# Normalised rows of seven groups turned by VectorE in 32x32 tiles, from pieces laid in place, where TensorE transposed them

## The chip, the core and the metric

The kernel runs on one core of a Trainium2 chip. The metric is the device time of one execution in microseconds (us). Engines are named as the profile names them: PE is TensorE (its weight loads are PEld), DVE is VectorE, ACT is ScalarE, POOL is GpSimd, SP is SyncE, which issues most of the transfers. A quadrant is 32 of the 128 partitions.

## What is computed

Linear attention, a Fourier mix over both axes, a layer norm without weights, and a two-layer network, all in float32; batch 8, 8 heads, 576 tokens, 64 features a head, so 512 features.

```python
k_s = softmax(k, axis=2)                     # over the tokens
kv = einsum('bhsd,bhse->bhde', k_s, v)
x = einsum('bhsd,bhde->bhse', softmax(q, axis=-1), kv)   # then (B, S, 512)
u = x + real(fft(fft(x, axis=1), axis=2))
un = (u - mean(u)) / sqrt(var(u) + 1e-06)    # over the 512 features
out = u + maximum(un @ w_ch1, 0) @ w_ch2     # 512 -> 2048 -> 512
```

## The kernel before

The 4608 rows are taken in nine groups of 512: group g (0 to 7) has 512 of the 576 rows of batch element g, and a last group, number 8, has the 64 left over of each. The order is 0 to 6, 8, 7. A position in this order is called an order below. For each group the network is done by Strassen products: a first layer (`up`, L1322; its products are L1334), one level deep, and a second (`down`, `deep_down`, L1383; products L1431 and L1461, and for order 1 L1550), two levels deep from order 2 on. While PE does the network of one group, the other engines and gaps in PE's row prepare the next group: keys, queries, values, the Fourier mix, and the norm. So there are hand-overs, at which PE goes from the last L1461 of one group to the first L1334 of the next.

The order of the work is written out by hand. Every step is put into one list with a time in units, the list is sorted (L1719), and each engine executes its own steps in that order; only data and buffers make it wait. One unit is a pair of products, and a group after the second one takes 56 units of `up` and 50 of `down`. `timed` (L1628) puts the parts of the preparation at their places, counted from the start of a group's `up` or `down`.

The norm (`norm`, L1156) works on four tiles of 128 rows by 512 features, u by another name x, in the order 0, 2, 1, 3:

- DVE takes statistics (L1165, L1166). ACT loads its table and takes the root of all four variances (L1169). DVE makes the scales and biases (L1172, L1173).
- ACT normalises a tile in one instruction, 128x512, with scale and bias read per row from memory (L1189).
- PE transposes it in four parts of 128x128 into PSUM (L1195), and ACT copies them from there into `unT` (L1204), which has the features on the partitions. A tile with number i = c + 2u fills half the columns of two of the blocks of `unT`.
- DVE and POOL make the differences that the Strassen products need (`combine`, L1210; `combine_last`, L1215). The second product of the next `up` reads block 5, the second of DVE's two differences. Then ACT loads the table of the exponential again (`back`, L1180).

`unT` has one buffer, `eo`, which holds the normalised tiles, has six.

Inside the second layer, products add up in PSUM banks ba, bb and bc, one buffer each. ACT copies the first product out of ba (s1, L1475) and later the sum in it (L1482); DVE reads bb for the sums u2, u3 and the result (L1468) and bc after them. A product that adds to bb, or starts a bank anew, waits for these reads. DVE also makes the sums of weights' counterparts for the next unit (L1407), POOL some of them, and adds results into x (L1411).

The keys of the next group but one (`keys`, L686) begin 7 units before a hand-over: key maxima on DVE (L695), exchanges between partitions on ACT and minima on DVE (L675, L678, L682), exponentials on ACT (L699), turns in 32x32 tiles on DVE (L708), products with the values on PE (L715), which `scale` (L721 to L725) divides. The queries go a like way: DVE turns them (L764), and ACT takes exponentials in 16 pieces of 32 partitions by 128 elements, each written to the quadrant where its features belong (L774). The new values of the other half are loaded by `values_to` (L648), the keys by `keys_to` (L638).

Of the kernel before, what the change touches and what calls it, by code (L numbers as in the profile page):

```python
# [40 lines left out]
F32 = mybir.dt.float32  # L41
I32, U32 = mybir.dt.int32, mybir.dt.uint32
ACT = mybir.ActivationFunctionType
ALU = mybir.AluOpType
AX = mybir.AxisListType

P = 128
B, H, S, DH = 8, 8, 576, 64
D = H * DH
# [3 lines left out]
HD = D // 2  # L53
# [5 lines left out]
Q = 32  # L59
W = 2 * Q  # L60
NT = Q // 2 + 1
KT = D // P
VD = 4 * NC - S // Q
NF = FF // P
GT = 4 * P
# [53 lines left out]
def at(t, script):  # L119
    return [(t + dt, step) for dt, step in script]  # L120
# [17 lines left out]
class _Block:  # L138
    def __init__(self, ctx, tc, q, kT, v, w1, w2, ft, cd, out):
# [24 lines left out]

        self.ZT = c.tile([P, KT, P], F32, name="ZT")

# [57 lines left out]
    def turned(self):  # L224
        t = self.ps.tile([P, 4, P], F32, tag="tr", name="tr", bufs=2)
        return t
# [102 lines left out]
    def weights(self):  # L329
# [6 lines left out]
        def fetch(i):  # L336
# [10 lines left out]
            if i < NF:  # L347
                nc.sync.dma_start(raw.rearrange("p (k n) -> p k n", k=KT), w1[:, :, f * 2 * P:(f + 1) * 2 * P])
            else:
# [129 lines left out]
    def attention_timed(self, b, start, end):  # L479

        tail = [("t", b)] if b % 2 == 0 else []
        own = [("q", b, c, u) for c, u in ((0, 0), (0, 1), (1, 1), (1, 0))]
        places, shared = [6, 13.5, 21.5, 27.2], start + 12
        if tail:
            places = [8.5, 14, 21.5, 27.2]
        if start == 0:
            places, shared = [13.5, 20.5, 24, 27.2], 7
        steps = at(start, self.keys(b))
        for it in tail:
            steps += at(shared, self.q_exp(it)) + at(shared + 8, self.t_turn(it))  # L490
            steps += at(22.4 if start < 0 else 35, self.t_fold(it))
        for t, it in zip(places, own):
            steps += at(t, self.own_exp(it)) + at(t + 15, self.own_times_kv(it))
        loads = [(t - 7, t + 7.6, self.own_load(it)) for t, it in zip(places, own)]
        loads += [(shared - 13, shared + 8.4, self.t_load(it)) for it in tail]
        loads.sort(key=lambda s: s[0])
        free = [-99] * 3
        for i, (t, end, load) in enumerate(loads):
            if i > 1:
                steps += at(max(t, free[-3]), load)  # L500
            free.append(end)
        return steps + at((33 if start < 0 else 39) if tail else max(22, start + 26), self.t_times_kv(b))

    def ahead(self, b):


        steps = at(24 if b > 2 else 20, self.keys_to(b))
        steps += at(35 if b > 2 else 22.5, self.values_to(b, 0))
        q = [self.own_load(("q", b, 0, u)) for u in range(2)]
        if b % 2 == 0:  # L510
            q = [self.t_load(("t", b)), q[0]]
        return steps + at(46.5, q[0]) + at(50, q[1])
# [170 lines left out]

        return [(0, copies), (0.3 + 0.15 * (4 // by), least)]

    def keys(self, b):  # L686


        nc, V, kb = self.nc, self.nc.vector, self.kb
        box = {}  # L690

        def top(r):
            if r == 0:
                box["m"] = self.small.tile([P, 4 * NR], F32, tag="km16", name="km16", bufs=2)
            V.reduce_max(box["m"][:, 4 * r:4 * r + 4], kb[:, r], axis=AX.X, negate=True)  # L695

        def exp(g):
            k = kb[:, g // 4, g % 4]
            nc.scalar.activation(k, k, ACT.Exp, bias=box["m"][:, g:g + 1])  # L699

        def turn(r):
            if r == 0:
                t = self.work.tile([P, KT, HD], F32, tag="Z", name="Z", bufs=1)
                t = t[:].rearrange("p k n -> p (k n)")[:, 0:NC * P]
            else:
                t = kb[:, r - 1].rearrange("p g s -> p (g s)")
            to = box["k", r] = t.rearrange("p (c n) -> p c n", n=P)
            V.transpose(to.rearrange("p c (g s) -> p c g s", s=Q), kb[:, r].rearrange("p g (c s) -> p c g s", s=Q))  # L708

        def times(r):  # L710
            pk, k = self.acc((P, P + 1)), box.pop(("k", r))
            box[r] = pk
            a = (P + 1) * (r % 2)
            for c in range(NC):
                nc.tensor.matmul(pk, lhsT=k[:, c, :], rhs=self.vt[:, c, a:a + P + 1], start=c == 0, stop=c == NC - 1)  # L715

        def scale(r):
            pk = box.pop(r)
            rec = self.small.tile([P, 1], F32, tag="krec", name="krec", bufs=4)
            at = P * (r % 2)  # L720
            V.tensor_scalar(out=rec[:], in0=pk[:, at:at + 1], scalar1=ATT_EPS, scalar2=None, op0=ALU.add)  # L721
            V.reciprocal(rec[:], rec[:])
            for h in range(2):
                s, cols = slice(64 * h, 64 * h + 64), slice(64 * h + 1 - r % 2, 64 * h + 65 - r % 2)
                V.tensor_scalar(out=self.kvr[b % 2][s, r, s], in0=pk[s, cols], scalar1=rec[s, 0:1], scalar2=None, op0=ALU.mult)  # L725

        steps = [(0.9 * r, lambda r=r: top(r)) for r in range(NR)]
        steps += at(3.6, self.across(lambda: box["m"], 2, 4 * NR)) + at(4.5, self.across(lambda: box["m"], 1, 4 * NR))
        steps += [(6 + g / 2, lambda g=g: exp(g)) for g in range(4 * NR)]
        for r in range(NR):  # L730
            for dt, f in ((8.3, turn), (10.8, times), (12.5, scale)):
                steps.append((dt + 2 * r + 6 * (r > 1 and f != turn), lambda f=f, r=r: f(r)))
        steps += at(13.5, self.values_to(b, 1))
        return steps

    def own_load(self, it):
# [419 lines left out]
    def norm(self, g):  # L1156

        nc, V = self.nc, self.nc.vector
        mv = self.small.tile([P, 4, 2], F32, tag="mv", name="mv", bufs=2)
        std = self.small.tile([P, 4], F32, tag="std", name="std", bufs=2)  # L1160
        uns, box = {}, {}
# [36 lines left out]
        def laid(i):  # L1198
# [4 lines left out]
            copy = V.tensor_copy if g == 0 and c == u else nc.scalar.copy  # L1203
            copy(self.unT[g][:, u:u + 3:2, :, cols], box.pop(i)[:].rearrange("p (a k) t -> p a k t", a=2))  # L1204

        def combine():
            if g > 0:
                some = lambda i: self.unT[g][:, i]
                for e, to, x, y in ((V, 4, 1, 0), (nc.gpsimd, 1, 3, 1), (V, 5, 3, 4)):
                    e.tensor_tensor(out=some(to), in0=some(x), in1=some(y), op=ALU.subtract)  # L1210
# [3 lines left out]
                some = lambda i: self.unT[g][:, i]  # L1214
                V.tensor_tensor(out=some(6), in0=some(2), in1=some(5), op=ALU.subtract)  # L1215

        steps = []
        put = lambda t, f, *a: steps.append((t, lambda: f(*a)))
        if g == 0:
            for some in ((0, 2), (1, 3)):  # L1220
                s = slice(some[0], 4, 2)
                for i in some:
                    put(0, stats, i)
                for f in (root, scales):
                    put(0, f, s)
        else:
            for n, i in enumerate((0, 2, 1, 3)):
                put((0.7, 2.7, 4.7, 6)[n], stats, i)
            s = slice(0, 4)
            put(7.2, root, s)  # L1230
            put(9, scales, s)
            put(13.6, back)
        for n, i in enumerate((0, 2, 1, 3)):
            put(9.3 + 1.3 * n, normal, i)
            put(11.8 + 1.3 * n, turn, i)
            put(12.6 + 1.3 * n, laid, i)
        put(17.5, combine)
        put(27.5, combine_last)
        return steps

    def plain(self, g, unT):
# [382 lines left out]
def kernel(ctx: ExitStack, tc: tile.TileContext, q, kT, v, w1, w2, ft,  # L1624
                                                           cd, out):
    blk = _Block(ctx, tc, q, kT, v, w1, w2, ft, cd, out)

    def timed(t, order, g):  # L1628
        b = order + 1
        steps = at(t, blk.up(order, g)) + at(t + UP, blk.down(g, order))  # L1630
        if order == B:
            return steps + [(t + 6 + 1.2 * i, lambda i=i: blk.later and blk.later.pop(0)()) for i in range(36)]
        if b == B:
            return steps + at(t + UP + 14, blk.norm(groups[b]))
        start, end = -7 if order > 2 else 0, 45
        if b + 1 < B:
            steps += at(t, blk.ahead(b + 1))
        steps += at(t, blk.attention_timed(b, start, end)) + at(t + end, blk.folded(b))
        t += UP
        for i, k in enumerate((2, 3, 0, 1, 4)):  # L1640
            steps += at(t + 2 + 2 * i, blk.block(b, k))
        mixes = [blk.mix_own(b, c) for c in range(2)]
        if b % 2:
            mixes.insert(0 if b == B - 1 else 2, blk.mix_shared(b // 2))
        for i, some in enumerate(mixes):
            steps += at(t + 12.5 + 3.2 * i, some)
        return steps + at(t + 29, blk.norm(groups[b]))

    fetch, convert = blk.weights()

# [26 lines left out]
    groups = [*range(B - 1), B, B - 1]  # L1677
    first, second, both = 46.9, 56, 77
    steps = blk.opening(fetch, converted)
# [3 lines left out]
    t = first + second  # L1683
# [26 lines left out]
    scale, before = 0.87, t + both  # L1710
    later = []
    t = 0
# [62 lines left out]
```

## Time and profile before

| what | value |
|---|---|
| median of three runs | 1055.6 us (1055.06 to 1058.19) |
| profiled execution | 1057.53 us, its span 1055.8 us |
| granted clock of PE over the span | 0.998 |
| busy: DVE, ACT, POOL | 722.6, 456.1, 406.0 us |
| PE transposes of the norms (L1195) | 144 of 128x128, 21.4 us of busy time, pipelined |
| normalising on ACT (L1189) | 34 tiles of 128x512, about 0.81 us each |
| copies to `unT` on ACT (L1204) | 34 tiles, 0.58 us each |
| hand-overs (first L1334 after L1461 or L1550) | 300.90, 414.82, 526.72, 638.79, 750.50, 863.01, 957.66 us |
| end of the scales before them (L1173) | 283.75, 403.16, 514.65, 627.13, 738.43, 851.24, 932.35 us |

The row of a group gives the line of the kernel, the engine, the operation, what is written and read, its shape and count; then its busy time and the mean ns of one, and the idle time of its engine just before with what ended it. A row of a timeline gives start and length in us, and in brackets the idle time before it.

### The profile page before, as it was taken

To read this page: it belongs to the slowest core of one execution; us is meant where nothing else is said; L and a number is where in the kernel's file an instruction comes from. 1 tells how busy PE (TensorE), PEld (TensorE's weight loads), DVE (VectorE), ACT (ScalarE), POOL (GpSimd) and SP (SyncE) were. 2 spreads that over 40 slices of the span, in tenths; PEclk is the share of its full clock that TensorE was granted. 3 is DMA by queue.
4 is the path that set the end of the run, shared out by engine and by line. 5 is a ranking of instruction groups with operands and counts; after the bars stand their busy time and mean duration, and the time that the engine had idled before them with its cause. 6 is when DMAs were issued, how large, how long until landed. Compare 5 with 4: busy or idle time off the path is not lost.

```text
span 1055.8 us, 16768 instructions
## 1 busy us (share of the span) xinstructions
PE 1037.7 (98%) x6178; PEld 899.8 (85%) x6178; DVE 722.6 (68%) x1410; ACT 456.1 (43%) x1141; POOL 406.0 (38%) x350
## 2 busy tenths in 40 slices
PE   8999999899999999999999999999999999999998
PEld 7844555788888899889998999989998998999898
DVE  6898888665566876767765777688657644674563
ACT  5674433672248316751476236821682132131210
POOL 3164320257415645465545643474446450000000
PEclk9999999999999999999999999999999999999999
DMA  9787598586998666855677467757644664576464
GB/s 269 240 281 258 164 257 273 167 251 197 300 308 242 206 217 243 230 190 210 251 236 220 179 239 238 206 201 260 212 170 162 229 243 165 206 259 221 173 222 147
DMA packets 114313, 236.01 MB, mean 224 GB/s; under 512 B 23272, under 2 KB 78696, under 8 KB 103608
## 3 DMA queue, kind: packets, MB, share of 16 engines
q1 hardware_dynamic: 113864, 234.42, 67.7%
q8 instruction: 49, 0.80, 0.3%
q14 instruction: 32, 0.26, 0.1%
q10 hardware_dynamic: 288, 0.26, 0.1%
q0 software_dynamic: 80, 0.26, 0.1%
HBM read 199.79 MB, written 39.06 MB: 226 GB/s over the span
## 4 chain that ended last, share of the span: by engine, by line
PE 78%; DVE 5%; ACT 4%; DMA 3%; issue 1%; SPq 0%; POOL 0%; DVEq 0%; ACTq 0%
PE bb L1334 14%; PE bb L1461 10%; PE ba L1334 10%; PE bc L1334 9%; PE bc L1461 7%; PE ba L1461 7%; PE bb L1431 5%; PE acc L715 3%; ACT qT L774 2%; PE bb L1550 2%; PE acc L790 2%; PE acc L1087 1%; PE acc L1090 1%; DMA vt<-in_v_dram 1%; PE bc L1550 1%; PE ba L1550 1%
## 5 line engine op out<-in xcount | busy, mean ns | idle before, releaser
L1334 PE MATMUL bb<-unT,big 128*128 128x256 f32 x768 | 183.1, 381 | 0.1
L1334 PEld LDWEIGHTS bb<-unT,big 128*128 128x128 f32 x768 | 144.7, 191 | 19.9 <-DVE u L1304 1.0
L1346 ACT ACTIVATE big<-big 128x512 f32<-128x512 f32 x96 | 60.3, 629 | 170.8 <-DVE big L1345 169.9
L1334 PE MATMUL ba<-unT,big 128*128 128x256 f32 x512 | 124.0, 379 | 0.2 <-ACT big L1341 0.2
L774 ACT ACTIVATE qT<-q 32x128 f32<-32x128 f32 x384 | 117.9, 307 | 12.1 <-DVE q L764 7.1
L1334 PE MATMUL bc<-unT,big 128*128 128x256 f32 x512 | 121.8, 380 | 0.5 <-DVE big L1345 0.5
L1304 DVE TENSOR_TENSOR u<-bb,s 128x512 f32<-128x512 f32 x66 | 45.4, 687 | 94.5 <-PE bb L1334 79.5
L1334 PEld LDWEIGHTS bc<-unT,big 128*128 128x128 f32 x512 | 96.1, 190 | 14.2 <-DVE big L1345 1.8
L1334 PEld LDWEIGHTS ba<-unT,big 128*128 128x128 f32 x512 | 94.8, 190 | 12.6 <-ACT big L1341 0.6
L1461 PE MATMUL bb<-big 128*128 128x128 f32 x848 | 105.1, 275 | 0.3 <-DVE u L1468 0.3
L1461 PEld LDWEIGHTS bb<-big 128*128 128x128 f32 x848 | 99.6, 192 | 0.5 <-DVE u L1468 0.4
L1411 POOL TENSOR_TENSOR x<-x,big 128x512 f32<-128x512 f32 x45 | 57.7, 1296 | 63.5 <-DVE big L1468 31.2
L1461 PE MATMUL ba<-big 128*128 128x128 f32 x640 | 79.6, 275 | 0.0
L1461 PEld LDWEIGHTS ba<-big 128*128 128x128 f32 x640 | 76.3, 192 | 1.2
L1407 DVE TENSOR_TENSOR big<-big 128x512 f32<-128x512 f32 x98 | 75.3, 806 | 0.0
L761 POOL TENSOR_TENSOR q<-q,qm 128x512 f32<-128x512 f32 x24 | 25.8, 1073 | 116.1 <-DVE qm L756 73.0
L1210 POOL TENSOR_TENSOR unT<-unT 128x512 f32<-128x512 f32 x8 | 14.1, 1769 | 124.6 <-DVE unT L1210 124.6
L1468 DVE TENSOR_TENSOR u<-bb,s 128x256 f32<-128x256 f32 x40 | 16.8, 420 | 64.8 <-PE bb L1461 61.5
L1431 PE MATMUL bb<-big 128*128 128x256 f32 x256 | 58.7, 381 | 0.0
L384 POOL TENSOR_TENSOR big<-big 128x512 f32<-128x512 f32 x24 | 30.4, 1268 | 71.0 <-ACT big L1346 71.0
L1345 DVE TENSOR_TENSOR big<-bc,u 128x512 f32<-128x512 f32 x64 | 44.0, 687 | 18.6 <-PE bc L1334 17.8
L1431 PEld LDWEIGHTS bb<-big 128*128 128x128 f32 x256 | 48.2, 190 | 8.0 <-DVE big L1345 1.1
(279 smaller groups left out, 2032.2 us busy)
## 6 DMA issues: line engine op xcount, KB each, us to landing
big<-w2d SPq DMA_DIRECT2D x67, 1024.0 KB
big<-w1s SPq DMA_DIRECT2D x64, 896.0 KB
big<-w2s SPq DMA_DIRECT2D x16, 1024.0 KB
big<-in_w_dram SPq DMA_DIRECT2D x21, 512.0 KB
w2d<-big SPq DMA_DIRECT2D x42, 256.0 KB
kb<-in_kT_dram SPq DMA_DIRECT2D x24, 320.0 KB
q<-in_q_dram SPq DMA_DIRECT2D x28, 256.0 KB
vt<-in_v_dram SPq DMA_DIRECT2D x36, 160.0 KB
```

The costliest lines, as they stand in the source:

```text
L384: e1.tensor_tensor(out=to(4), in0=at(2), in1=at(3), op=ALU.add)
L715: nc.tensor.matmul(pk, lhsT=k[:, c, :], rhs=self.vt[:, c, a:a + P + 1], start=c == 0, stop=c == NC - 1)
L774: nc.scalar.activation(to[t, i * Q:i * Q + Q], one, ACT.Exp)
L1304: plus = lambda t: V.tensor_tensor(out=temp(t), in0=box["bb"][:], in1=box["s1"][:], op=ALU.add)
L1334: nc.tensor.matmul(bank()[:, i, :], lhsT=w[:, WA_AT[m], k * P:(k + 1) * P], rhs=self.unT[g][:, B_AT[m], k, :], start=first and i == 0 and ...
L1345: steps = [(0, lambda: V.tensor_tensor(out=hp(i), in0=bank()[:], in1=u()[:], op=ALU.add)), (0.8, lambda: nc.scalar.activation(hp(i), hp(i) ...
L1346: (0.8, lambda: nc.scalar.activation(hp(i), hp(i), ACT.Relu))]
L1407: e.tensor_tensor(out=to(o), in0=to(x), in1=to(y), op=op)
L1411: E.tensor_tensor(out=x, in0=x, in1=tile(m), op=ALU.add)
L1431: nc.tensor.matmul(box[name][:, i, :], lhsT=h[p][:, A_AT[m], i * P:(i + 1) * P], rhs=self.stream[n][:, p, :], start=p == 0 and (m != 1 or ...
L1461: nc.tensor.matmul(box[place[n]][:, i, :], lhsT=own(m)(A_AT[n])[:, f, :], rhs=w[:, r // 2, r % 2 * P:r % 2 * P + P], start=first and f == ...
L1550: nc.tensor.matmul(bank()[:, i, :], lhsT=h[p][:, A_AT[m], i * P:(i + 1) * P], rhs=w[:, p, :], start=first and i == 0 and p == 0, stop=p == ...
```

## The change

For groups 2 to 6, 8 and 7 (all from order 2 on) PE's transposes and ACT's copies go. A tile is normalised in 16 pieces of 32 rows by 128 elements: from quadrant j of the rows, those 32 features of each block of 128 that belong on quadrant t are written to quadrant t, at the place of rows j (`spread`). Six of the 16 (ON_DVE) are done by DVE and ten by ACT; in group 7 ACT does all. Then DVE turns the whole tile in 32x32 tiles straight into `unT` (`turned`). The norm begins 24 units after the start of `down` where it began at 29 (14, as before, in group 7); its differences keep their place, and come 6 units later in group 7. Products and scales of the keys come 1.5 units later, those of the last two quarters in orders 1 and 2 3.5; loads of values 1.5 later; loads of keys 3 later for two groups; the products of shared rows up to 3 later.

```diff
+ON_DVE = (2, 5, 7, 10, 13, 15)
-        steps = at(start, self.keys(b))
+        steps = at(start, self.keys(b, start))
-        return steps + at((33 if start < 0 else 39) if tail else max(22, start + 26), self.t_times_kv(b))
+        return steps + at((33 if start < 0 else 39) if tail else max(22, start + 29), self.t_times_kv(b))
-        steps = at(24 if b > 2 else 20, self.keys_to(b))
+        steps = at(20 if b == 2 else 27 if b < 5 else 24, self.keys_to(b))
-            for dt, f in ((8.3, turn), (10.8, times), (12.5, scale)):
-                steps.append((dt + 2 * r + 6 * (r > 1 and f != turn), lambda f=f, r=r: f(r)))
-        steps += at(13.5, self.values_to(b, 1))
+            for dt, f in ((8.3, turn), (12.3, times), (14, scale)):
+                steps.append((dt + 2 * r + (6 + 2 * (start == 0)) * (r > 1 and f != turn), lambda f=f, r=r: f(r)))
+        steps += at(15, self.values_to(b, 1))
+        def spread(i, some):
+            x = self.xpart(g, i % 2, i // 2).rearrange("p (k t s) -> t p k s", k=KT, t=4)
+            if i not in uns:
+                uns[i] = self.halves()
+            to = uns[i][:, 0:D].rearrange("p (k j s) -> j p k s", k=KT, j=4)
+            for n in some:
+                j, t = n // 4, n % 4
+                r = slice(j * Q, j * Q + Q)
+                one, y = x[t, r], to[j, t * Q:t * Q + Q]
+                if n in ON_DVE and g != B - 1:
+                    V.tensor_scalar(out=y, in0=one, scalar1=std[r, i:i + 1], scalar2=mv[r, i, 0:1], op0=ALU.mult, op1=ALU.add)
+                else:
+                    nc.scalar.activation(y, one, ACT.Identity, bias=mv[r, i, 0:1], scale=std[r, i:i + 1])
+        def turned(i):
...
+            c, u = i % 2, i // 2
+            V.transpose(self.unT[g][:, u:u + 3:2, :, c * P:c * P + P], uns[i][:, 0:D].rearrange("p (a k t) -> p a k t", a=2, k=2))
-        steps = []
+        steps, each = [], 2.75 if g < B - 1 or g == B else 4.4
-            put(13.6, back)
+            put(13.6 if g < 2 else 9.5 + 4 * each, back)
         for n, i in enumerate((0, 2, 1, 3)):
-            put(9.3 + 1.3 * n, normal, i)
-            put(11.8 + 1.3 * n, turn, i)
-            put(12.6 + 1.3 * n, laid, i)
-        put(17.5, combine)
-        put(27.5, combine_last)
+            if g < 2:
...
+                continue
+            for k in range(8):
+                put(9.3 + each * n + each / 8 * k, spread, i, (2 * k, 2 * k + 1))
+            put(10.25 + each * (n + 1), turned, i)
+        late = 5 * (g > 1) + 6 * (g == B - 1)
+        put(17.5 + late, combine)
+        put(27.5 + late, combine_last)
-        return steps + at(t + 29, blk.norm(groups[b]))
+        return steps + at(t + 24, blk.norm(groups[b]))
```

More of the change, by code (lines that the diff above doesn't have):

```diff
@@ L684, in across, with keys @@
         return [(0, copies), (0.3 + 0.15 * (4 // by), least)]
-    def keys(self, b):
+    def keys(self, b, start):
         nc, V, kb = self.nc, self.nc.vector, self.kb
@@ L1204, in laid @@
             copy(self.unT[g][:, u:u + 3:2, :, cols], box.pop(i)[:].rearrange("p (a k) t -> p a k t", a=2))
+        def spread(i, some):
[12 more added lines that the diff above has]
+        def turned(i):
+            if g not in self.unT:
+                self.unT[g] = self.work.tile([P, 7, 2, HD], F32, tag="unT", name="unT", bufs=1)
+            c, u = i % 2, i // 2
+            V.transpose(self.unT[g][:, u:u + 3:2, :, c * P:c * P + P], uns[i][:, 0:D].rearrange("p (a k t) -> p a k t", a=2, k=2))
         def combine():
@@ L1231, in norm @@
             put(9, scales, s)
-            put(13.6, back)
+            put(13.6 if g < 2 else 9.5 + 4 * each, back)
         for n, i in enumerate((0, 2, 1, 3)):
-            put(9.3 + 1.3 * n, normal, i)
-            put(11.8 + 1.3 * n, turn, i)
-            put(12.6 + 1.3 * n, laid, i)
-        put(17.5, combine)
-        put(27.5, combine_last)
+            if g < 2:
+                put(9.3 + 1.3 * n, normal, i)
+                put(11.8 + 1.3 * n, turn, i)
+                put(12.6 + 1.3 * n, laid, i)
+                continue
[5 more added lines that the diff above has]
+        put(27.5 + late, combine_last)
         return steps
```

## The prediction

> **What bounds it now.** I read the engine shares first, then the forms of the groups on ScalarE and TensorE, then the timeline around one hand-over from a group's last products to the next group's first, 490 to 545 us (the hand-over into group 4).
>
> ```profile
> PE 1037.7 (98%) x6178; PEld 899.8 (85%) x6178; DVE 722.6 (68%) x1410; ACT 456.1 (43%) x1141; POOL 406.0 (38%) x350
> ```
>
> TensorE has work in 98% of the span, so whatever leaves it is worth its full time, and any microsecond in which it waits is added. ACT's 43% is a mean over stages. What the change does is decided in the some 12 us before each hand-over. PE's timeline there (start, length, line, operands):
>
> ```profile
> 516.04 1.06 PE L1461 MATMUL bc<-big 128*128 128x128 f32 x8
> 516.94 0.60 PE L1195 MATMUL tr<-ident,eo 128*128 128x128 f32 x4
> 517.37 1.06 PE L1461 MATMUL bc<-big 128*128 128x128 f32 x8
> 518.27 1.06 PE L1461 MATMUL bb<-big 128*128 128x128 f32 x8
> ...
> 524.94 1.95 PE L1461 MATMUL bc<-big 128*128 128x128 f32 x16
> 526.72 1.89 PE L1334 MATMUL ba<-unT,big 128*128 128x256 f32 x8
> 528.45 1.89 PE L1334 MATMUL bb<-unT,big 128*128 128x256 f32 x8
> ```
>
> Starts follow starts without a hole: four transposes take 0.43 us of the row (516.94 to 517.37), a product of two halves 1.79, a product of the next layer 1.73. DVE and ACT in the same stretch:
>
> ```profile
> 507.74 0.41 DVE L1468 TENSOR_TENSOR u<-bb,s 128x256 f32<-128x256 f32 x1
> 508.19 0.42 DVE L1468 TENSOR_TENSOR big<-bc,u 128x256 f32<-128x256 f32 x1
> 508.53 0.68 DVE L1165 BATCH_NORM_STATS2 st<-x 128x6 f32<-128x512 f32 x1
> ...
> 513.50 1.16 DVE L1173 SCALAR_TENSOR_TENSOR mv<-mv,std 128x4 f32<-128x4 f32 x1
> 516.31 0.42 DVE L1468 TENSOR_TENSOR u<-bb,s 128x256 f32<-128x256 f32 x1 [1.66 <-ACT eo L1189]
> ```
> ```profile
> 514.51 0.37 ACT L1475 COPY s<-ba 128x256 f32<-128x256 f32 x1 [1.26 <-PE ba L1461]
> 514.78 2.23 ACT L1189 ACTIVATE eo<-x,mv,std 128x512 f32<-128x512 f32 x3
> ...
> 523.35 0.37 ACT L1482 COPY big<-ba 128x256 f32<-128x256 f32 x1 [1.64 <-PE ba L1461]
> ```
>
> The scales end at 513.50 + 1.16 = 514.66; the next layer starts at 526.72. All of the normalising must fit between, and PE needs three services of ACT and DVE meanwhile: the copy of s (L1475) and the sum u (L1468), which reads bank bb before it is written again, and L1482, which frees bank ba.
>
> **Removed.** 16 transposes for each of 7 groups, 112 by 0.109 us (0.43 over 4): 12.2 us of PE, 1.75 a group. Four L1189 and four L1204 go from ACT.
>
> **Added on ACT.** 40 pieces of 32x128 a group (64 in group 7, which is normalised last, where DVE takes none). No row has such a piece; these are nearest:
>
> ```profile
> L774 ACT ACTIVATE qT<-q 32x128 f32<-32x128 f32 x384 | 117.9, 307 | 12.1 <-DVE q L764 7.1
> L904 ACT ACTIVATE q<-q 128x512 f32<-128x512 f32 x4 | 2.5, 630 | 10.0 <-POOL q L900 10.0
> L1189 ACT ACTIVATE eo<-x,mv,std 128x512 f32<-128x512 f32 x30 | 23.0, 809 | 3.4 <-DVE mv L1173 3.4
> L854 ACT ACTIVATE q<-q,qm 128x64 f32<-128x64 f32 x24 | 6.5, 334 | 0.3 <-DVE qm L848 0.3
> ```
>
> L774 has the shape, but neither a scale nor a bias in memory. The same 512 elements take 809 ns with both (L1189) and 630 with neither (L904): 179 ns more. That this is per instruction and not per element is borne out by the bias: at 0.84 ns an element (630 less 307 over 384), L854's 64 elements should take 253, and take 334. So a piece takes 307 + 179 = 486 ns. Six L774 in a row take 1.89 us, 0.32 each, so each is its own length and some 11 ns apart: a = **0.497 us**. The bounds are 0.319 (L774 as it is) and, if pieces overlap as three L1189 do (2.23 us, 0.71 apart), 0.715 less 384 by 0.84 ns, 0.39. I take 0.497, since the piece has L774's partitions and L1189's operands.
>
> [...]
>
> **Added on DVE.** A tile's six pieces, and a turn of 0.71 (L764). A piece lies between L721's 139 ns (128x1, no operand in memory) and L1186's 530 (the same operation on 128x512); nearest is L725, 284 for 64x64 with one operand, so I take 0.3. A tile then costs 2.5 us, at most 3.9, less than its ten ACT pieces at 5.0, which cover it: no cost. Without that cover it would be 10 us of DVE a group.
>
> **Moved.** The statistics go 5 units earlier (a group of 106 units takes 112 us, so 5.3 us), but DVE is busy without a hole from the last addition to x (502.3) to the scales: they can pass only the two L1468 of 0.34 and 0.39 that stood between them. Pieces start at S = 514.66 - 0.7 = 513.95. Three statistics at 0.82 now stand ahead of the L1468 at 507.74, 2.5 us that PE must wait out too, but within the longer wait below. The keys' products come later by 1.5 units and the last two of order 1 and 2 by 3.5: PE waits 2.65 us at 200.9 for a load of v, which lands at 203.5; asked for 3.7 later, with the load itself about one issue later, 2.2 us of it goes (bounds 0 and 2.65). The loads of keys move by 3 units past one load of weights in SP's queue and are used some 70 units later; the products of the shared rows move by 3 units and are used 30 later: 0.
>
> **The new wait.** ACT's order in the changed program: root, L1482, 17 pieces, L1475, 23 pieces, table load and root (1.5 us), L1482. DVE's: the turn of the third tile waits for 30 ACT pieces, and behind it stand a piece, a key maximum (0.73), a piece and the last u (L1468), for which PE's bank bb waits. Two ways to the next layer's first product:
> - by u: S + 30a + 0.3 (L1475) + 2.45 on DVE + two products, 3.6 = S + 30a + 6.35;
> - by bank ba: S + 40a + 0.3 + 1.5 + 0.4 (L1482) = S + 40a + 2.2.
>
> With a = 0.497 the second is later: S + 22.1. Before, the layer started 12.4, 12.8, 12.4 and 12.8 after S into groups 3, 4, 5 and 6, and 12.5 into the group of shared rows: later by 9.7, 9.3, 9.7, 9.3 and 9.6, **47.6** (the 1.75 is in it, as PE stands still anyway). Into group 2 the products before it are longer. The scales ended at 283.75 there; with the statistics out of the way they come right behind the L1565 that ends at 281.4, S = 281.75. Then 40a, and 3.9 on DVE (turn 0.7, two differences of 1.25, the L1565 that frees bank bb, 0.7): 305.5, where PE's second product began at 302.63: **+2.9**. Into group 7: 932.35 + 64a + 0.9 of copies + 3.0 (turn, two differences, L1411, u) = 968.0 where PE wrote bb at 954.08: **+14.0**. Sum 64.5 less 2.2: **+62**. Key products may be up to 1.7 late behind ACT at four hand-overs; taken as 0, kept as 7 for the range.
>
> The profiled execution took 1057.5 (span 1055.8), 1.9 over the median; against the median 1055.6 + 62 = **1118**.
>
> **Rivals.**
> 1. *Pieces overlap* (0.39): by u, 5.7, 5.3, 5.7, 5.3; shared 5.3; group 2 -1.4; group 7 +7.1; less 2.2: +31, 1086. For it L1189's spacing, against it L774's.
> 2. *The operands cost nothing* (0.319): by u 3.6, 3.2, 3.6, 3.2, 2.5; group 2 -1.75; group 7 +2.6; less 2.2: +15, 1070. Against it L854.
> 3. *Faster: the statistics really come 5 us earlier.* If DVE gets past its L1407 in time (POOL's work beside it stretches some to 0.87 and more), so that S is 4.6 earlier, and a is 0.319, then 30a + 6.35 = 15.9 fits into 12.4 + 4.6 = 17.0: 1.1, 1.4, 1.1 and 1.4 are won into groups 3 to 6, the full 1.75 into 2 and 8, group 7 still loses 2.6, and 2.2 more is won: -8.5, 1047. It decides from S 3.6 earlier on. Against it: DVE has no hole there.
> 4. That PE keeps its transposes is excluded: its order in the changed program has none for these groups.
>
> **Chances.** Forecast 0.60, rival 1 0.14, rival 2 0.10, rival 3 0.10, between or beyond 0.06. The range 1066 to 1130 leaves out rival 3 and what is beyond the late keys. Faster by over 0.3% (about what a measurement of this kernel tells from no change) 0.11, within 0.03, slower 0.86.
>
> **What would show it.** Right: pieces of about 486 ns at 0.5 apart, ACT full for 20 us before each hand-over, PE waiting for L1482's and L1468's successors, each hand-over some 9 later, PE under 95%. Wrong: pieces near 0.3, S several us earlier, PE without a hole.

## The result: 1119.2 us, 6% slower

The changed kernel takes **1119.24 us**, median of 4 runs (1118.02 to 1120.93), against 1055.46 for the kernel before: a ratio of 1.060, interval 1.0576 to 1.0623. Its profiled execution has a span of 1118.1 where before had 1055.8, so 62.3 us are to be found. The view below gives the engine shares of the profile after, and then its chain that ended last, by engine and by line:

```profile
PE 1049.3 (94%) x6066; PEld 907.1 (81%) x6066; DVE 802.3 (72%) x1582; ACT 568.5 (51%) x1389; POOL 405.7 (36%) x350
...
PE 48%; ACT 13%; DVE 11%; issue 2%; DMA 1%; SPq 0%; DVEq 0%; ACTq 0%
PE bb L1361 12%; ACT eo L1219 11%; PE bc L1361 8%; PE ba L1361 7%; PE bb L1458 5%; PE bb L1488 4%; PE bc L1488 3%; PE ba L1488 2%; DVE big L1434 2%; PE acc L791 2%; PE acc L716 1%; DVE st L1166 1%; PE acc L1088 1%; PE acc L1091 1%; PE acc L1116 1%
```

PE fell from 98% to 94%, and one line of ACT, the pieces (L1219), holds 11% of the chain. (Lines move by about 27: L1334, L1461, L1468, L1475, L1482 of before are L1361, L1488, L1495, L1502, L1509 after.) The hand-over into group 4, PE's timeline (start, length, line, operands, in brackets the idle time before and what ended it):

```profile
530.60 3.78 PE L1488 MATMUL bb<-big 128*128 128x128 f32 x16 [4.07 <-DVE u L1495]
534.17 3.12 PE L1488 MATMUL ba<-big 128*128 128x128 f32 x16
537.73 2.05 PE L1488 MATMUL bb<-big 128*128 128x128 f32 x16 [0.44 <-DVE u L1495]
539.62 1.95 PE L1488 MATMUL bc<-big 128*128 128x128 f32 x16
541.81 1.99 PE L1361 MATMUL ba<-unT,big 128*128 128x256 f32 x8 [0.24 <-ACT big L1509]
544.75 1.99 PE L1361 MATMUL bb<-unT,big 128*128 128x256 f32 x8 [0.95 <-DVE big L1495]
```

ACT and DVE in the same stretch:

```profile
519.45 8.55 ACT L1219 ACTIVATE eo<-x,mv,std 32x128 f32<-32x128 f32 x17 [0.30 <-DVE mv L1174]
528.02 0.37 ACT L1502 COPY s<-ba 128x256 f32<-128x256 f32 x1
528.41 11.56 ACT L1219 ACTIVATE eo<-x,mv,std 32x128 f32<-32x128 f32 x23
540.00 1.28 ACT L1181 ACT_TABLE_LOAD   x1
541.29 0.20 ACT L1181 ACTIVATE root<-std 128x1 f32<-128x1 f32 x1
541.40 0.35 ACT L1509 COPY big<-ba 128x256 f32<-128x256 f32 x1
```
```profile
519.25 0.16 DVE L1174 SCALAR_TENSOR_TENSOR mv<-mv,std 128x4 f32<-128x4 f32 x1
...
525.95 4.13 DVE L1217 TENSOR_SCALAR eo<-x,std,mv 32x128 f32<-32x128 f32 x6
530.12 0.42 DVE L1495 TENSOR_TENSOR u<-bb,s 128x256 f32<-128x256 f32 x1
...
534.97 0.71 DVE L1225 STREAM_TRANSPOSE unT<-eo 128x512 f32<-128x512 f32 x1 [1.65 <-ACT eo L1219]
```

Read ACT's block from the top: the scales end at 519.41, 17 pieces, the copy of s, 23 pieces, table load, root, and the copy that frees bank ba, which ends at 541.75; PE's next layer begins at 541.81. ACT has no hole in these 22.4 us. PE stops twice for a sum u in them (4.07 and 0.44) and 0.24 for bank ba, and behind the first stop 16 products last 3.78 and 3.12 us where 1.95 is usual. The two stops differ. The first u, at 530.12, stands behind six DVE pieces of 4.13 in all, and DVE did not wait for ACT ahead of it. The second stands behind the turn of the third tile, which waited 1.65 for ACT. The groups of pieces (busy time and mean ns of one behind the bar):

```profile
L1219 ACT ACTIVATE eo<-x,mv,std 32x128 f32<-32x128 f32 x264 | 129.1, 489 | 10.9 <-DVE mv L1174 7.1
...
L1217 DVE TENSOR_SCALAR eo<-x,std,mv 32x128 f32<-32x128 f32 x120 | 58.4, 487 | 2.4
```

From hand-over to hand-over (first product of the next group to first product of the one after), us of the profiled executions; the last column but one belongs to the first experiment:

| stretch that ends | before | after | moves alone | after less before |
|---|---|---|---|---|
| into group 2 | 121.34 | 113.75 | 115.51 | -7.6 |
| into group 3 (has group 2's first wait) | 113.92 | 129.06 | 112.65 | +15.1 |
| into group 4 | 111.90 | 120.55 | 111.34 | +8.7 |
| into group 5 | 112.06 | 122.21 | 111.90 | +10.2 |
| into group 6 | 111.72 | 120.55 | 111.34 | +8.8 |
| into the shared rows | 112.51 | 122.92 | 112.34 | +10.4 |
| into group 7 | 94.64 | 112.36 | 94.64 | +17.7 |
| at the end | 98.10 | 98.25 | 98.24 | +0.2 |

The last column adds up to 63.5; what lies ahead of the first of these stretches is 1.1 shorter.

### The profile page after: what moved, and what is told of

The parts are those of the page before. It is cut to its first block, busy times and chain, and to the rows that moved or that the text cites. A ratio compares the mean times of both kernels' runs of the same rounds, so it can differ in the third digit from the quotient of the medians.

```text
span 1118.1 us, 17000 instructions
## 1 busy us (share of the span) xinstructions
PE 1049.3 (94%) x6066; PEld 907.1 (81%) x6066; DVE 802.3 (72%) x1582; ACT 568.5 (51%) x1389; POOL 405.7 (36%) x350
## 4 chain that ended last, share of the span: by engine, by line
PE 48%; ACT 13%; DVE 11%; issue 2%; DMA 1%; SPq 0%; DVEq 0%; ACTq 0%
PE bb L1361 12%; ACT eo L1219 11%; PE bc L1361 8%; PE ba L1361 7%; PE bb L1458 5%; PE bb L1488 4%; PE bc L1488 3%; PE ba L1488 2%; DVE big L1434 2%; PE acc L791 2%; PE acc L716 1%; DVE st L1166 1%; PE acc L1088 1%; PE acc L1091 1%; PE acc L1116 1%
## 5 line engine op out<-in xcount | busy, mean ns | idle before, releaser
L1361 PE MATMUL bb<-unT,big 128*128 128x256 f32 x768 | 184.5, 383 | 11.0 <-DVE x L1592 4.7
L1361 PEld LDWEIGHTS bb<-unT,big 128*128 128x128 f32 x768 | 145.0, 191 | 33.1 <-DVE big L1495 5.4
L1488 PE MATMUL bb<-big 128*128 128x128 f32 x848 | 118.5, 298 | 42.4 <-DVE u L1495 42.4
L1488 PEld LDWEIGHTS bb<-big 128*128 128x128 f32 x848 | 111.0, 211 | 46.4 <-DVE u L1495 45.8
L1219 ACT ACTIVATE eo<-x,mv,std 32x128 f32<-32x128 f32 x264 | 129.1, 489 | 10.9 <-DVE mv L1174 7.1
L1361 PE MATMUL ba<-unT,big 128*128 128x256 f32 x512 | 124.5, 380 | 2.0 <-ACT big L1509 2.0
L1361 PE MATMUL bc<-unT,big 128*128 128x256 f32 x512 | 122.9, 382 | 0.0
L1361 PEld LDWEIGHTS bc<-unT,big 128*128 128x128 f32 x512 | 96.9, 192 | 13.9 <-DVE big L1372 0.7
L1361 PEld LDWEIGHTS ba<-unT,big 128*128 128x128 f32 x512 | 94.4, 190 | 15.0 <-ACT big L1509 3.0
L1488 PE MATMUL ba<-big 128*128 128x128 f32 x640 | 82.5, 283 | 0.0
L1488 PEld LDWEIGHTS ba<-big 128*128 128x128 f32 x640 | 80.0, 201 | 1.4 <-ACT big L1509 0.2
L1438 POOL TENSOR_TENSOR x<-x,big 128x512 f32<-128x512 f32 x45 | 57.6, 1295 | 62.9 <-DVE big L1495 24.2
L1434 DVE TENSOR_TENSOR big<-big 128x512 f32<-128x512 f32 x98 | 69.4, 740 | 0.0
L1217 DVE TENSOR_SCALAR eo<-x,std,mv 32x128 f32<-32x128 f32 x120 | 58.4, 487 | 2.4
```

Of the source, the lines that this page charges most:

```text
L1217: V.tensor_scalar(out=y, in0=one, scalar1=std[r, i:i + 1], scalar2=mv[r, i, 0:1], op0=ALU.mult, op1=ALU.add)
L1219: nc.scalar.activation(y, one, ACT.Identity, bias=mv[r, i, 0:1], scale=std[r, i:i + 1])
L1361: nc.tensor.matmul(bank()[:, i, :], lhsT=w[:, WA_AT[m], k * P:(k + 1) * P], rhs=self.unT[g][:, B_AT[m], k, :], start=first and i == 0 and ...
L1434: e.tensor_tensor(out=to(o), in0=to(x), in1=to(y), op=op)
L1438: E.tensor_tensor(out=x, in0=x, in1=tile(m), op=ALU.add)
L1488: nc.tensor.matmul(box[place[n]][:, i, :], lhsT=own(m)(A_AT[n])[:, f, :], rhs=w[:, r // 2, r % 2 * P:r % 2 * P + P], start=first and f == ...
```

## The experiments

The theory is the prediction's: 40 pieces on ACT, half a us each, stand between the scales and the copy that PE waits for, and DVE's pieces lie beneath them. Rivals: the pieces' operands are what costs (rival 2 of the prediction, turned round), DVE is the bound, the TensorE clock makes the loss, or the moves have a part in it. Ratios are to the kernel before, run on the same chip beside each.

**1. The moves alone.** The kernel before with only the diff's other moves: key products, loads of keys and values, and shared rows:

```diff
-        steps = at(start, self.keys(b))
+        steps = at(start, self.keys(b, start))
-            for dt, f in ((8.3, turn), (10.8, times), (12.5, scale)):
+            for dt, f in ((8.3, turn), (12.3, times), (14, scale)):
...
```

> The kernel before, with only the moves of the change: products and scales of the keys, loads of keys and of values, products of the shared rows. The norm is as before. My theory (these moves pay by themselves, through the wait for the load of v in order 1): the wait of 2.65 us goes, and the products that ran at half clock behind it (1.1 us more than usual) with it, 0.8 more of small waits; 4 to 5 us faster, about 1051. Rival (in the changed kernel order 1 is 7.6 us shorter because of the norm alone): 1055, no change.

Measured: 1049.28 (8 runs), ratio 0.9949, interval 0.9931 to 0.9966: 5.6 us faster than the kernel before on the same chip. PE at the place of the wait for v, before and then in this run:

```profile
203.53 2.39 PE L715 MATMUL acc<-vt,kb 128*128 128x129 f32 x10 [2.65 <-DMA vt<-in_v_dram]
205.71 1.70 PE L1334 MATMUL bb<-unT,big 128*128 128x256 f32 x4
```
```profile
202.59 1.28 PE L715 MATMUL acc<-vt,kb 128*128 128x129 f32 x10
203.71 1.03 PE L1334 MATMUL bb<-unT,big 128*128 128x256 f32 x4
```

The wait is gone, and ten products take 1.28 where they took 2.39 behind it: a wait of 2.65 cost more than its length. The view of windows shows why (columns: PE, PEld, DVE, ACT, POOL busy, granted TensorE clock, share of DMA, GB/s), before:

```profile
203.60:207.00 3.40, 3.40 (x14) 3.13 (x15) 0.00 (x0) 0.00 (x0) 0.33 (x1) 0.51 0.28 114
```

The granted clock stood at half for 3.4 us behind that wait. Which of the moves takes the wait away was not separated.

**2. The other half.** The changed kernel with these moves undone:

```diff
-            for dt, f in ((8.3, turn), (12.3, times), (14, scale)):
+            for dt, f in ((8.3, turn), (10.8, times), (12.5, scale)):
...
```

> The changed kernel with the moves of the key products, the values and the shared rows undone: the normalising alone is changed. If the two parts add up, it gives back the 5.6 us that the moves alone took from the kernel before: 1125. If the waits that the pieces make cover the wait for v and what goes with it, 1119. If the key products of the old places now wait behind ACT's pieces as well, 1127 or more.

Measured: 1125.56 (4 runs), ratio 1.0655, interval 1.0624 to 1.0685. The two parts add up: the moves give 5.6 without the new normalising and 6.3 with it; the normalising alone costs some 70. The four runs lie in two pairs (1122.7 and 1122.8, 1128.3 and 1128.9), so the 6.3 is rough, and the waits behind it are not the same: in this run's trace the place of the wait for v has a wait of 1.58 with the clock at full, and the half clock follows a wait of 2.01 earlier, at 165.93.

**3. Plain pieces on ACT.**

```diff
-                    nc.scalar.activation(y, one, ACT.Identity, bias=mv[r, i, 0:1], scale=std[r, i:i + 1])
+                    nc.scalar.copy(y, one)
```

> The changed kernel, with each of ACT's pieces a plain copy without scale and bias; it leaves out the normalising of the rows and columns that ACT does. Theory (the length of ACT's pieces, 0.50 us apart, decides): pieces some 0.32 apart take the way by u, S + 15.9 instead of S + 22.4, 6.5 less at five hand-overs, some 8 less into group 2 (its wait and the half clock behind it), 14 less into group 7: about 1065. Rival (DVE's pieces and turns, or the statistics ahead of the sums u, are what PE waits for): over 1105.

Measured: 1093.97 (2 runs), ratio 1.0371, interval 1.0339 to 1.0403. Neither time came: the pieces fell to 295 ns, 0.307 apart, but only 25 us came back. ACT's second block, DVE's u and PE into group 4:

```profile
517.51 7.07 ACT L1219 COPY eo<-x 32x128 f32<-32x128 f32 x23
```
```profile
518.78 4.13 DVE L1217 TENSOR_SCALAR eo<-x,std,mv 32x128 f32<-32x128 f32 x6
522.95 0.42 DVE L1495 TENSOR_TENSOR u<-bb,s 128x256 f32<-128x256 f32 x1
```
```profile
523.42 3.17 PE L1488 MATMUL bb<-big 128*128 128x128 f32 x16 [4.07 <-DVE u L1495]
```

ACT's copy of s is done before its second block, at 517.5, and u comes at 522.95 all the same: six pieces of DVE stand ahead of it and take 4.13. With ACT shorter, DVE is the bound.

**4. and 5. A square of four: DVE's pieces plain, with ACT's plain and with ACT's as they are.**

```diff
-                    V.tensor_scalar(out=y, in0=one, scalar1=std[r, i:i + 1], scalar2=mv[r, i, 0:1], op0=ALU.mult, op1=ALU.add)
+                    V.tensor_copy(y, one)
```

> The changed kernel with all pieces as plain copies, on ACT (as in the run that gave 1094) and on DVE too: it leaves out the normalising of u in groups 2 to 8. It asks what held the hand-overs 7 to 8.5 late once ACT's pieces were 0.31 apart. If it is the length of DVE's 24 pieces with two operands (352 ns apart at best, 487 on the mean), plain ones, by L721's 139 ns for the smallest copy some 0.2 to 0.25 apart, save 3 to 5 us at each of five hand-overs: 1070 to 1079. If it is the queue on DVE (a turn that waits for ACT with the last u behind it), whatever the length of a piece: 1090 to 1094.

> The changed kernel with DVE's 144 pieces as plain copies (216 to 220 ns) and ACT's as they are: it leaves out the normalising of those six pieces of each tile. With the changed kernel (1119), the one with plain ACT pieces (1094) and the one with both plain (1083) it makes a square of four. By the prediction's step (ACT's pieces cover DVE's, which cost nothing): 1117 to 1119. If what DVE's pieces take stands in the path beside ACT's, since the turn and the last u are queued behind them, they give what they gave between the other two, 11: 1108.

Measured, us:

| | DVE's pieces with operands | plain |
|---|---|---|
| ACT's pieces with operands | 1119.2 | 1118.85 (4 runs) |
| plain | 1094.0 | 1082.9 (2 runs) |

The upper row settles it: shorter pieces on DVE alone give nothing (ratio 1.0596, interval 1.0564 to 1.0629). Their cover is ACT, as the prediction had it, and a turn waits for ACT again with the last u behind it (PE and DVE in the run with DVE's alone plain):

```profile
540.15 3.12 PE L1488 MATMUL bb<-big 128*128 128x128 f32 x16 [3.89 <-DVE u L1495]
```
```profile
537.63 0.71 DVE L1225 STREAM_TRANSPOSE unT<-eo 128x512 f32<-128x512 f32 x1 [2.91 <-ACT eo L1219]
...
539.67 0.42 DVE L1495 TENSOR_TENSOR u<-bb,s 128x256 f32<-128x256 f32 x1
```

At three of the five hand-overs the next layer starts 22.4 behind the scales, as in the changed kernel. At the other two the products behind this stop, partly at half clock (into group 4, 16 of them take 3.12 us and the next 16 take 2.56, where 1.95 is usual), end later than bank ba is free, and the layer starts 23.4 and 24.0 behind them.

In the lower row, without that cover, they are worth 11 us. With both plain 28 us remain, between the two numbers expected of that run. Its DVE, and POOL beside it:

```profile
512.70 4.87 DVE L1217 COPY eo<-x 32x128 f32<-32x128 f32 x6
517.60 0.42 DVE L1495 TENSOR_TENSOR u<-bb,s 128x256 f32<-128x256 f32 x1
...
518.66 1.40 DVE L1217 COPY eo<-x 32x128 f32<-32x128 f32 x6
```
```profile
511.96 1.27 POOL L1438 TENSOR_TENSOR x<-x,big 128x512 f32<-128x512 f32 x1
513.19 1.26 POOL L1441 TENSOR_TENSOR big<-big 128x512 f32<-128x512 f32 x1
514.53 2.48 POOL L1438 TENSOR_TENSOR x<-x,big 128x512 f32<-128x512 f32 x2
```

Six copies take 1.40 with POOL idle and 4.87 beside the end of one POOL instruction and three whole ones; the three copies that meet the whole ones last 1.21, 1.33 and 1.21 where 0.22 is usual. So a short piece of DVE can last about as long as the POOL instruction that it meets (1.21 to 1.33 us here beside 1.24 to 1.27), and making it shorter doesn't help there. How the rest of the 28 us divides wasn't tried.

**6. The norm at 29 again.** The changed kernel with the old start of the norm, its pieces closer, the last turn where it was. (With the old start alone the last turn would stand at 50.25 units, behind the 50 of `down`; there is no time for that kernel.)

```diff
-        return steps + at(t + 24, blk.norm(groups[b]))
+        return steps + at(t + 29, blk.norm(groups[b]))
-        steps, each = [], 2.75 if g < B - 1 or g == B else 4.4
+        steps, each = [], 1.5 if g < B - 1 or g == B else 4.4
-        late = 5 * (g > 1) + 6 * (g == B - 1)
+        late = 11 * (g == B - 1)
```

> The changed kernel with the normalising begun 29 units into the order as before, not 24, its pieces spaced more closely so that the last turn keeps its place. It measures what the 5 units buy. If the scales end 3.6 us sooner by them, as the two traces read (12.3 us from the last addition to the scales before, 8.8 after), five hand-overs come 3 to 3.6 later each: 1134 to 1138. By the prediction's sizing (0.7 each): 1123. If a queue behind the pieces and not their start sets the hand-over: 1119.

Measured: 1134.28 (4 runs), ratio 1.0757, interval 1.0732 to 1.0782. The time is that of the first theory, but by its traces the size at each hand-over is not: reckoned from the hand-over before, the scales into groups 4, 5, 6 and the shared rows end 2.1, 2.2, 3.1 and 1.8 later than in the changed kernel, 2.3 on the mean, and the stretches into group 2 (0.6), group 3 (1.7) and group 7 (1.8) grow as well. The layer then starts 22.0 to 23.1 behind the scales, much as after. ACT here, all 40 pieces in one block:

```profile
524.71 20.12 ACT L1219 ACTIVATE eo<-x,mv,std 32x128 f32<-32x128 f32 x40
```

**7. The clock kept up.** Small products with the identity into a bank that nobody reads, ahead of the waiting product at two places:

```diff
+    def awake(self, n):
+        t = self.turned()
+        for _ in range(n):
+            self.nc.tensor.matmul(t[:, 0, :], lhsT=self.ident[:], rhs=self.ident[:], start=True, stop=True)
...
+            if order == 2 and j == 0:
+                steps.append((1.9, lambda: self.awake(20)))
...
+                if order_at == B - 1 and i == 3 and o == 4:
+                    put(t + 2 * k - 0.05, self.awake, 18)
```

> The changed kernel, with 20 and 18 small products of the identity with itself, into a bank that nobody reads, ahead of two products that PE waits for: the second of the layer into group 2, and the one behind the last u before group 7. Theory (the wait itself brings PE's clock down to half, and what follows runs at half for some us): no half clock there, 3.3 + 1.7 = 5 us less, about 1114, though the products lie inside waits of 4.7 and 4.6 us. Rival (the half clock has another cause, or its loss is hidden): 1119 or a little more.

Measured: 1116.57 (4 runs), ratio 1.0587, interval 1.0561 to 1.0613. The window behind the wait into group 2, after and then this run (granted clock the third number from the end):

```profile
297.70:304.50 6.80, 5.71 (x14) 4.55 (x15) 5.89 (x11) 1.21 (x6) 1.56 (x1) 0.50 0.93 298
```
```profile
297.70:304.50 6.80, 5.48 (x28) 4.45 (x27) 5.86 (x11) 1.21 (x6) 1.43 (x1) 1.00 0.92 286
```

The half clock is gone at both places and the two stretches are 1.9 and 1.5 shorter (127.14, 110.82), 3.4 together where 5 was expected. The intervals of the two kernels overlap, so it is the stretches and not the total that show it. At these two places the clock makes a few us of the loss, not the loss; the other half-clock stretches were left as they are.

**8. Group 7 spread.** The changed kernel with group 7's 64 pieces laid over the whole order before it, where ACT has holes:

```diff
+        if g == B - 1:
+            for n, i in enumerate((0, 2, 1, 3)):
+                for m in range(16):
+                    put(14 + 13.5 * n + 0.84 * m, spread, i, (m,))
+                put(UP + 27 - 20 + 2 * n, turned, i)
...
-            return steps + at(t + UP + 14, blk.norm(groups[b]))
+            return steps + at(t + 20, blk.norm(groups[b]))
```

> The changed kernel with group 7 alone laid out as in the run that spread its 64 pieces over the whole of its order. It measures the term of group 7 (predicted +14.0, by the trace +17.7). Order 7 should fall from 112.4 to the 93.5 it has where the pieces are spread: 1100 to 1101. If something else than the pressed pieces makes that order long (DVE's work, or a TensorE clock that falls in the waits before it): 1105 to 1119.

Measured: 1101.13 (4 runs), ratio 1.0436, interval 1.0404 to 1.0467. The stretch into group 7 falls from 112.36 to 93.59, and the 64 pieces are the same. Not only they have moved: the whole norm of group 7 begins 50 units earlier, its statistics too, so that the scales end 26.2 behind the hand-over where they ended 69.4, and the three half-clock stretches of that order are gone with the waits. ACT after, in one press, and then here:

```profile
978.38 14.06 ACT L1219 ACTIVATE eo<-x,mv,std 32x128 f32<-32x128 f32 x28
992.46 0.37 ACT L1509 COPY big<-ba 128x256 f32<-128x256 f32 x1
992.86 11.06 ACT L1219 ACTIVATE eo<-x,mv,std 32x128 f32<-32x128 f32 x22
```
```profile
939.99 0.49 ACT L1219 ACTIVATE eo<-x,mv,std 32x128 f32<-32x128 f32 x1
940.39 0.57 ACT L1376 ACTIVATE big<-ba 128x512 f32<-128x512 f32 x1
940.98 1.50 ACT L1219 ACTIVATE eo<-x,mv,std 32x128 f32<-32x128 f32 x3
```

**9. Is there a version that beats both?** The moves alone with group 7, and only group 7, laid out so (the diffs of 1 and 8 on the kernel before; the expected text of experiment 8 refers to this run):

> The kernel before with the moves of the key products, the values and the shared rows alone (the run that gave 1049.3), and group 7 alone laid out by pieces: all 64 of its pieces on ACT as in the change, but begun with the order of group 7 itself, one every 0.84 units, the four turns on DVE where its transposes were read, its 16 transposes gone from PE. Theory (what costs the change its time is that the pieces are pressed into the stretch between the scales and the next group's first product): ACT has over 40 us idle in that order, the 64 pieces of 0.50 take 32 of them, nothing waits, and PE keeps the 1.75 us: 1047.5, ratio to the run with the moves alone 0.998. Rival (pieces cost wherever they stand, since ACT's copies for PE queue behind them, half a piece, 0.25 us, on each of some 20 copies): 1050 to 1054.

Measured: 1048.34 (5 runs), ratio 0.9932, interval 0.9917 to 0.9947. It beats the kernel before and the changed one, but not measurably the moves alone (0.9931 to 0.9966): the theory's 1.75 us show as 1.2 in the stretch into group 7 (93.47 against 94.64), too little for these totals. Against the rival: nothing was lost.

## Why the prediction was right

It said 1118; 1119.2 came. Step by step:

- **The piece on ACT, 486 ns, 0.497 apart: right.** 489, and 0.503 in blocks (8.55 over 17, 20.12 over 40). L774's shape with L1189's operands was the right pair of rows. Plain pieces take 295 where 307 was taken and the two operands 194 where 179 was taken, two small errors that cancel. Rival 1 (overlap) falls with it.
- **The way by bank ba, S + 22.1: right.** 22.4 from the scales to the next layer at all five hand-overs from group 3 to the shared rows, in the order that was written down (17 pieces, s, 23 pieces, table, root, copy), and at all five PE waits for that copy last. The margin is small: into group 4 PE had the products behind the last u done 0.24 before bank ba was free. The first stop of PE, 4.07 for the u ahead of the last, was not in the prediction; it lies within the 22.4 and costs nothing there.
- **ACT covers DVE: right in result, wrong in price.** A piece of 0.3 was taken; it takes 340 ns, 352 apart, 487 on the mean, since beside POOL some take up to 1.45 us. It costs nothing only because ACT is that slow (the square of four). Rival 2's 1070 was therefore too low: it supposed that u came by 30 pieces and 2.45 us of DVE, and with ACT's pieces at 0.307 the time is 1094.
- **The statistics' move, 0.7: mis-sized, and hidden.** It buys 2.3 (run 6). Part of what the prediction lacked stands in its own row 513.50: the last instruction of the scales takes 1.16 there, and 0.16 in the changed kernel (519.25). That is 1.0 less at all five hand-overs against the kernel before, and at three of the four compared here against run 6. But after the hand-over PE's second product waits 0.95 for a DVE addition (the line at 544.75), DVE's work behind it is late too (read from the traces, not tried), and about 1.3 of the 2.3 is given back (in run 6 the scales end 1.3 later, from the hand-over before, than in the kernel before). What is left is 0.2 to 1.7, mean 1.0. So +8.7, +10.2, +8.8, +10.4 came for +9.3, +9.7, +9.3, +9.6.
- **The wait for v, -2.2: mis-sized.** The moves are worth 5.6 to 6.3. The half clock behind the wait wasn't in the sum, though before's trace shows it (1.28 against 2.39 for the ten products).
- **Group 2, +2.9: mis-sized.** Against the moves alone the two stretches into groups 2 and 3 are 14.7 longer; less 9.8, the mean of the next four against the same run, 4.8 is group 2's. Half clock behind the wait of 4.70 makes 1.9 of it (run 7).
- **Group 7, +14.0: mis-sized, +17.7.** PE wrote bb 37.7 behind the scales where 35.7 was reckoned, the L1438 ahead of u taking 1.75 on DVE among the rest; and from there the layer came 5.2 later (before 3.6), at half clock (granted 0.50 from 1014.49 to 1017.90).
- **Late key products, 0: right.** In the changed kernel PE waits for them (L716) 0.39 us at most, for a load of v. With the old places, in run 2, it waits 1.05 us for a turned key block behind four hand-overs; the four stretches there are 0.5 longer on the mean.

The undersized gain of the moves (3.4) and the undersized losses in groups 2 and 7 (1.9 and 3.7) are of opposite sign; that the total is within 1.2 us is partly luck. Rival 3 needed pieces at 0.319 and S 3.6 earlier; with 0.307 in run 3 its place was still taken by DVE. (Its terms add up to -8.1, not to the -8.5 that the prediction gives.)

## What to carry to other kernels

An engine with half its time idle can still be the bound (ACT is busy 51% here): count what a change adds between the last input (the scales here) and the first consumer, and not against the share of the span. The same 64 pieces cost 18 us pressed into that stretch and nothing spread over an order with the scales made early. Where two engines share such work, shortening one shows only the other (here plain pieces on DVE alone gave nothing, 1118.85 against 1119.2, on ACT alone 25 us, on both 36): vary both before naming the bound.

## What was not expected of the hardware

- **A wait of PE can cost more than its length.** At each of the changed kernel's nine waits over 3 us (3.13 to 6.04) the granted clock is 0.50 for 3.41 or 6.83 us, within the wait or behind it; before has it once besides its end, at the wait of 2.65. Where PE waits again soon it is hidden (into group 4 PE waits 0.24 for bank ba all the same); behind the wait into group 2 and in group 7 it is on the path (1.9 and 1.5 us in run 7). The length of a wait alone does not tell: one of 2.65 was enough in the kernel before; the two of 1.86 in the changed kernel were not (16 products behind each take 2.05), nor was one of 3.25 in the run with DVE's pieces alone plain (2.05 and 1.95 behind it). In the changed kernel's trace the nine half-clock stretches begin whole multiples of 3.413 us from one another (112.64, 119.47, 122.88, 119.47, 122.88, 92.16, 13.65 and 13.65). In the 3.41 us ahead of each, PE waits 2.04 to 3.41 in all; of the other stretches of that length at full clock, counted off from the same places, none holds more than 1.83 of waits. What lies behind this, and where the limit is, was not tried.
- **Short pieces of DVE beside POOL** take up to 1.34 us plain and 1.45 with operands, for 0.22 and 0.34 alone. In the changed kernel's trace none of the 113 pieces that meet no POOL instruction takes over 0.36, and 27 of the 31 that meet one take over 0.4. In run 4 each copy that meets a whole POOL instruction, itself some 1.25 long, takes 1.0 to 1.1 us more than alone. What holds the pieces there no trace shows.
